# Attention decode with an FFN gate: K loaded ahead of V, the weights placed around them, PV later in the program

## Chip, cores and metric

The kernel runs on one core of a Trainium2 chip. The metric is the device time of one execution in microseconds (us), taken as the median over runs of the same build. The "span" in a profile runs from the first to the last profiled instruction; it lies about 1.8 us below the time of the same run (121.44 against 119.6 before).

Names used below: PE is the TensorE (matmuls and transposes), DVE the VectorE, ACT the ScalarE, SP the engine whose program issues nearly all loads (`SPq` in the views), in the order that is here called the queue. SBUF is the memory on the core, PSUM the one that PE writes to. PV is the product `p @ v`, the FFN is the two products with w1 and w2, and "S7" are the scores of pair 7, the last pair.

## The reference, cut to what matters

```python
# x: [2, 1, 448]; k_cache, v_cache: [2, 8, 8192, 256]; wq: [448, 4096]; wo: [4096, 448]; w1: [448, 1792]; w2: [1792, 448]
xn = layernorm(x)
q  = (xn @ wq) -> [2, 16 heads, 1, 256]
k, v = last 2048 positions of the caches, each of 8 KV heads shared by 2 query heads
p  = softmax(q @ k^T / 16)
s  = (p @ v) @ wo
g  = silu(relu(xn @ w1) @ w2)
out = x + s * g
```

All tensors are bf16. The work is small, the bytes are not: K and V windows 2 x 16.8 MB, wq and wo 2 x 3.7 MB, w1 and w2 2 x 1.6 MB, together 44.1 MB that are each read once.

## The kernel before

The eight KV heads are eight "pairs" (a K and a V of 2 MiB, each loaded as two transfers of 1 MiB, one per batch entry). Per pair, PE transposes K in eight steps (`do_T`), DVE or ACT copy each transposed chunk from PSUM to SBUF ("evacuation"), then come scores (`do_S`), softmax (`ch_*`), PV (`do_PV`, eight steps) and a small output transpose (`do_osb`, `do_oT`). The engines' programs are built step by step: step `8k+s` holds chunk `s` of K of pair `k`, and the other work is hung on later steps. What the whole document turns on: the engines work off these programs in order, so **a piece of work that must wait stops everything behind it on that engine** (the run a_pv_early shows it for PE: transposes whose data had landed stood still for 8.24 us).

```python
NKB, NVB = 3, 4              # buffers for K and V
def load_k(k): d_k[k] = [dma(SP, kbuf[k % NKB], K[k, b], after last_T[k - NKB]) for b in 0, 1]
def load_v(k): d_v[k] = [dma(SP, vbuf[k % NVB], V[k, b], after last_PV[k - NVB]) for b in 0, 1]
# start of the queue: K0 (four half transfers), wq, K1
...
def do_T(i):                 # four PE transposes of one chunk, then its evacuation
    deps = [*landed, p_idf, evac.get(i - 3)]
    ...
    if i % 2 == 0: evac[i] = DVE copy
    else:          evac[i] = ACT copy
...
def do_PV(k, n):             # four matmuls
    deps = [*d_v[k], st["pt", k], ...]
...
at_step(2, 1, do_xr)
at_step(NCH - 1, 1, do_q)                    # NCH = 8
at_step(5 * NCH + 2, 6, do_H)                # FFN: w1
at_step(5 * NCH + 4, 6, do_hT)
at_step(5 * NCH + 6, 6, do_F)                # FFN: w2
for k in range(8):
    e = NCH * k
    at_step(e + 8, 2, do_S(k, 0)); at_step(e + 9, 2, do_S(k, 1))
    at_step(e + 9, 4, ch_max); at_step(e + 11, 4, ch_rmT); at_step(e + 12, 4, ch_bias, ch_exp)
    at_step(e + 15, 4, ch_Pt); at_step(e + 15, 5, ch_sum)
    for n in range(8):
        at_step(e + 17 + n, 3, do_PV(k, n))
    at_step(e + 24, 5, do_osb); at_step(e + 25, 5, do_oT)
# order of the rest of the queue; wo comes last, in four parts
"v0 k2 v1 k3 v2 w1 k4 v3 w2 k5 v4 k6 v5 k7 v6 v7"
...
# after all pairs: at2 (two matmuls, two copies), 128 projection matmuls,
# out = sbk * g + x in two DVE operations, two output DMAs
```

Of the kernel before, what the change touches and what calls it, by code (L numbers as in the profile page):

```python
# [11 lines left out]
PE, DVE, ACTE, SP, POOL = "pe", "dve", "act", "sp", "pool"  # L12
# [64 lines left out]
def bass_recurrent_scan__sliding_block_cached__dense_activation_relu__decode_kernel(  # L77
# [12 lines left out]
    _, HKV, SK, DH = A_k_cache.shape  # L90
# [8 lines left out]
    NT = W // 64  # L99
    NPAIR = HKV  # L100
    NCH = 8
    SLOTS = 7
# [4 lines left out]
    HC = HD // 2  # L107
# [5 lines left out]
    with es:  # L113
        pr = _Prog(nc, es)
# [7 lines left out]
        def view(t, off, dims, n=128, p0=0, pstep=1):  # L122
            width = t.shape[1]
            return bass.AP(t, p0 * width + off, [[width * pstep, n]] + dims)
# [15 lines left out]
        xr = named("xr", [128, SLOTS * 4], BF)  # L140
# [18 lines left out]
        at2 = named("at2", [128, 64], BF)  # L159
        wqo = named("wqo", [128, 32 * D], BF)  # L160
# [3 lines left out]
        kbuf = [named(f"kbuf{i}", [128, NT * DH], BF) for i in range(NKB)]  # L164
# [8 lines left out]
        mbk = mb16[:, :].bitcast(F32).tensor  # L173

        def mbk_ap(lo, n, rows=128):
            return view(mbk, lo, [[1, n]], n=rows)

        def kv_src(k, b, cache):
            return cache[b, k, SK - W:SK, :].rearrange("(m t) d -> m (t d)", t=NT)
# [5 lines left out]
        d_k, d_v = {}, {}  # L185
# [7 lines left out]
        def load_k(k):  # L193
            d_k[k] = [pr.dma(SP, kv_dst(kbuf[k % NKB], b), kv_src(k, b, A_k_cache), [last_T.get(k - NKB)])
                      for b in range(2)]
# [2 lines left out]
            d_v[k] = [pr.dma(SP, kv_dst(vbuf[k % NVB], b), kv_src(k, b, A_v_cache), [last_PV.get(k - NVB)])  # L198
                      for b in range(2)]

        d_k[0] = {}
        for h in range(2):
            for b in range(2):
                lo = h * (NT // 2) * DH
                d_k[0][h, b] = pr.dma((SP, ACTE)[b] if h == 0 else SP,
                                      view(kbuf[0], lo, [[1, NT // 2 * DH]], n=64, p0=b, pstep=2),
                                      kv_src(0, b, A_k_cache)[:, lo:lo + NT // 2 * DH])
        d_x = pr.dma(ACTE, x_sb[0:B, :], A_x[:, 0, :])
        d_xc = [pr.dma(ACTE, view(x_c, 0, [[1, NCOL]], n=4, p0=b, pstep=32),
                       A_x[b, 0, :].rearrange("(i n) -> i n", i=4), [p_xc]) for b in range(B)]  # L210
        d_wq = pr.dma(SP, wqo[:, 0:SLOTS * HC], wq_src)
        load_k(1)

        i0 = pr.op(POOL, lambda e: e.memset(ident[:, :], 0.0))
        p_id = pr.op(POOL, lambda e: e.affine_select(
# [53 lines left out]
        def do_T(i):  # L269
            k, s = divmod(i, NCH)  # L270
            bank, src = tb[i % 3], kbuf[k % NKB]
            src_f, bank_f = src[:, :].bitcast(F32), bank[:, :].bitcast(F32)
            landed = [d_k[0][s // 4, b] for b in range(2)] if k == 0 else d_k[k]
            deps = [*landed, p_idf, evac.get(i - 3)]
            for n in range(4):
                lo = (4 * s + n) * (DH // 2)
                o = pr.op(PE, lambda e, n=n, lo=lo: e.matmul(  # L277
                    bank_f[:, n * 128:(n + 1) * 128], lhsT=src_f[:, lo:lo + 128], rhs=ident_f[:, :],
                    start=True, stop=True, is_transpose=True), deps)
                deps = []  # L280
            last_T[k] = o
            if s == NCH - 1:
                freed.add((load_k, k))
            dst = kt[(i // 2) % (NKT // 2)]
            dst = dst[:, 1024 * (i % 2):1024 * (i % 2) + 1024]
            deps = [o, last_S.get(i - NKT)]
            if i % 2 == 0:
                evac[i] = pr.op(DVE, lambda e: e.tensor_copy(dst, view(bank, 0, [[1, 4], [4, 256]])), deps)  # L288
            else:
                evac[i] = pr.op(ACTE, lambda e: e.activation(dst, view(bank, 0, [[1, 4], [4, 256]]), ACT.Copy), deps)  # L290
# [53 lines left out]
        def ch_sum(k):  # L344
            st["gs", k] = pr.op(PE, mm(mbk_ap(130, 1), gsum[:, :], ssum[k % 2][:, 0:1], True, True),
                                [st["mbk"], v_gs])
            st["rs", k] = st["mbk"] = pr.op(DVE, lambda e: e.reciprocal(rs[:, k:k + 1], mbk_ap(130, 1)), [st["gs", k]])  # L347

        def do_PV(k, n):
            bank, src, p = obk[k % 2], vbuf[k % NVB], pt[k % NP]  # L350
            deps = [*d_v[k], st["pt", k], a_z[2]] + ([st.get(("osb", k - 2)), st["q"]] if n == 0 else [])
            for i in range(4):
                lo = (8 * i + n) * DH
                o = pr.op(PE, mm(bank[32 * i:32 * i + 4, 0:DH], p[:, 16 * n + 4 * i:16 * n + 4 * i + 4],
                                 src[:, lo:lo + DH], n == 0, n == 7, tile_position=(0, 32 * i)), deps)
                deps = []
            last_PV[k] = o
            if n == 7:
                freed.add((load_v, k))

        def do_osb(k):
            st["osb", k] = pr.op(DVE, lambda e: e.tensor_scalar(  # L362
                out=o_sb[k % 2][:, :], in0=obk[k % 2][:, 0:DH], scalar1=rs[:, k:k + 1], scalar2=None, op0=ALU.mult),
                [last_PV[k], st["rs", k], st.get(("oT", k - 2))])
# [12 lines left out]
                    in1=view(qmask, 0, [[0, 2], [0, 2], [1, 4]]), op=ALU.mult), [o, v_qm])  # L377

        def do_q():
            deps = [d_wq, st["xr"], a_z[0]]  # L380
            for s in range(SLOTS):
                for i in range(4):
                    lo = s * HC + i * 512
                    o = pr.op(PE, mm(obk[0][32 * i:32 * i + 4, :], xr[:, 4 * s:4 * s + 4], wqo[:, lo:lo + 512],
                                     s == 0, s == SLOTS - 1, tile_position=(0, 32 * i)), deps)
                    deps = []
            st["q_mm"] = o
            v = pr.op(DVE, lambda e: e.tensor_scalar(
                out=q_n[:, :], in0=obk[0][:, :], scalar1=SCALE, scalar2=None, op0=ALU.mult), [o])
            deps = [v, st["xr"]]  # L390
            for n in range(4):
                o = pr.op(PE, lambda e, n=n: e.matmul(
                    mb16[:, 128 * n:128 * n + 128], lhsT=view(q_n, 256 * (n // 2) + n % 2, [[2, 128]]),
                    rhs=ident[:, :], start=True, stop=True, is_transpose=True), deps)
                deps = []
            for b in range(2):
                for r in range(2):
                    st["q"] = st["mbk"] = pr.op(DVE, lambda e, b=b, r=r: e.tensor_copy(
                        view(qz, 6 * b + r, [[64, 2], [16, 4], [8, 2]]),
                        view(mb16, 256 * r + b, [[2, 2], [32, 4], [128, 2]])), [o, p_qz])  # L400
# [48 lines left out]
        def at_step(i, order, fn):  # L449
            steps.setdefault(i, []).append((order, fn))  # L450

        for i in range(NCH * NPAIR):
            at_step(i, 0, lambda i=i: do_T(i))
        at_step(2, 1, do_xr)
        at_step(NCH - 1, 1, do_q)
        at_step(5 * NCH + 2, 6, do_H)
        at_step(5 * NCH + 4, 6, do_hT)
        at_step(5 * NCH + 6, 6, do_F)
        for k in range(NPAIR):
            e = NCH * k  # L460
            at_step(e + 8, 2, lambda k=k: do_S(k, 0))
            at_step(e + 9, 2, lambda k=k: do_S(k, 1))
            at_step(e + 9, 4, lambda k=k: ch_max(k))
            at_step(e + 11, 4, lambda k=k: ch_rmT(k))
            at_step(e + 12, 4, lambda k=k: ch_bias(k))
            at_step(e + 12, 4, lambda k=k: ch_exp(k))
            at_step(e + 15, 4, lambda k=k: ch_Pt(k))
            at_step(e + 15, 5, lambda k=k: ch_sum(k))
            for n in range(8):
                at_step(e + 17 + n, 3, lambda k=k, n=n: do_PV(k, n))  # L470
            at_step(e + 24, 5, lambda k=k: do_osb(k))
            at_step(e + 25, 5, lambda k=k: do_oT(k))

        loads = []
        for n in "v0 k2 v1 k3 v2 w1 k4 v3 w2 k5 v4 k6 v5 k7 v6 v7".split():
            if n[0] == "w":
                loads.append(((load_w1, load_w2)[int(n[1]) - 1], 0, 1))
            else:
                load, nb = (load_k, NKB) if n[0] == "k" else (load_v, NVB)
                loads.append((load, int(n[1]), nb))  # L480
# [14 lines left out]
        for b in range(2):  # L495
            m_at = pr.op(PE, mm(mbk_ap(256 + 32 * b, 32), at_exp[:, 128 * b:128 * b + 128],
                                fold[:, :], True, True), [st["at", NPAIR - 1, b], v_fold, st["mbk"]])
            v_at2 = st["mbk"] = pr.op(DVE, lambda e, b=b: e.tensor_copy(  # L498
                view(at2, b, [[2, 32]]), mbk_ap(256 + 32 * b, 32)), [m_at])
        deps = [v_at2, st["exp", NPAIR - 1]]  # L500
        landed = dict(d_wo)
        for j in range(32):
# [44 lines left out]
```

## Time and profile before

| | before |
|---|---|
| time, median of 4 runs | 121.57 us (121.25 to 121.86) |
| span of the profiled run | 119.6 us |
| bytes read | 44.1 MB |
| last byte landed | 108.3 us |
| K7 landed / V7 landed | 89.7 / 99.5 us |
| last K transpose done | 101.1 us |
| projection matmuls | 113.4 to 116.5 us |

The first view is the page of the kernel before. The rows of digits are 40 slices of 3 us; each digit is the busy share in tenths. `PEclk` is the clock that the TensorE was granted, in tenths.

```profile
span 119.6 us, 2338 instructions
...
PE   0091953697299989920999359995999899857490
...
PEclk9999679859958999995589985999679999996555
DMA  3998999999999999999999999999999999970000
...
DMA 43%; PE 34%; DVE 6%; ACT 5%; SPq 5%; issue 3%
```

The DMA row is full until slice 35, near 107 us, and then empty for four slices. So the kernel has two limits one after the other: the DMA engines up to 108 us, and then 11 us in which no input byte moves. The PE row has holes in slices 17 to 18 and 22 to 23 (counted from 0), and it is busy again at the end, when the DMA has nothing left to do.

The landing times of the transfers are not in a view of the page; I took them from the trace's records of DMA completions. On SP's queue they come strictly in issue order, one MiB every 2.45 us (428 GB/s). The Trainium skill (DMA: Bandwidth & Descriptors, "Queues, rings and completion order") says less than that: on an engine descriptors are consumed in ring order, but a later one may finish its write before an earlier one. The same page puts the fabric's ceiling at 435 GB/s ("Specifications"), so the queue runs within 2% of it.

The next view is the timeline of PE before, in order of time: start, duration, what ran, and in brackets how long PE sat idle before it and what the profile holds responsible.

```profile
51.42 0.38 PE L255 MATMUL mbk<-ssum,gsum 128*128 128x1 f32 x2 [0.38 <-DVE pt L339]
56.50 1.08 PE L277 MATMUL tb<-ident_f,kbuf 128*128 128x128 f32 x4 [4.69 <-issue]
...
66.73 0.38 PE L255 MATMUL mbk<-ssum,gsum 128*128 128x1 f32 x2 [0.39 <-DVE pt L339]
70.15 0.63 PE L277 MATMUL tb<-ident_f,kbuf 128*128 128x128 f32 x4 [3.04 <-issue]
```

The 4.69 and 3.04 us are put down to "issue", which means that the profile found no releaser. The landing records name it: the second halves of K4 and K5 landed at 56.41 and 70.06, less than 0.1 us before PE went on. (My prediction calls these two K3 and K4; counted from zero they are K4 and K5.) In the queue V2 and w1 stand before K4, and V3 and w2 before K5; a weight takes 3.83 us. The first four transposes of K4 take 1.08 us instead of 0.66: the granted clock was 0.5 there. (Those of K5 took 0.63; its second four took 1.12.)

The last view is the same timeline at the end of the kernel before:

```profile
93.57 0.63 PE L277 MATMUL tb<-ident_f,kbuf 128*128 128x128 f32 x4
...
100.44 0.66 PE L277 MATMUL tb<-ident_f,kbuf 128*128 128x128 f32 x4
...
102.29 0.39 PE L255 MATMUL sbk<-kt,qz 128*4 128x512 bf16 x3
102.84 0.59 PE L255 MATMUL sbk<-kt,qz 128*4 128x512 bf16 x5 [0.16 <-ACT kt L290]
...
107.37 0.36 PE L255 MATMUL mbk<-ident,e_sb 128*128 128x16 bf16 x8 [1.06 <-ACT e_sb L327]
...
109.54 1.67 PE L255 MATMUL obk<-vbuf,pt 128*4 128x256 bf16 x28
...
112.36 0.21 PE L255 MATMUL mbk<-fold,at_exp 128*128 128x32 bf16 x1 [0.35 <-DVE at_exp L374]
...
113.36 3.16 PE L255 MATMUL sbk<-wqo,at 128*2 128x112 bf16 x128 [0.29 <-DVE at L498]
```

`tb<-ident_f,kbuf` are the first and the last transposes of K7, `sbk<-kt,qz` the scores of pair 7, `mbk<-ident,e_sb` the transposes of its probabilities, `obk<-vbuf,pt` PV7, `sbk<-wqo,at` the projection. No line here waits for a DMA: V7 has lain there since 99.5 and wo since 108.3. PE and its partners work off, one after the other, what the late K7 left.

### The profile page before, as it was taken

How to read it: one execution, taken by the hardware profiler on the slowest of the kernel's cores; microseconds unless marked ns; L12 is line 12 of the kernel's file. 1: busy time of each engine (PE TensorE's matmuls, PEld its weight loads, DVE VectorE, ACT ScalarE, POOL GpSimd, SP SyncE). 2: the span in 40 equal slices, each digit the busy share in tenths (PEclk: the TensorE clock that was granted, in tenths of full speed). 3: DMA queues.
4: the chain of work that ended last, by engine and by line, in shares of the span. 5: the costliest groups of instructions: out<-in, count | busy, mean ns of one | idle time of the engine just before them, and what ended most of it. 6: DMA issues, size and time to landing. Idle time of an engine off the chain costs nothing.

```text
span 119.6 us, 2338 instructions
## 1 busy us (share of the span) xinstructions
PE 85.6 (72%) x1015; PEld 53.5 (45%) x1015; DVE 62.9 (53%) x124; ACT 45.6 (38%) x56; POOL 1.8 (2%) x13
## 2 busy tenths in 40 slices
PE   0091953697299989920999359995999899857490
PEld 0081931466145655611456225574466566324280
DVE  0059743449246778720567335886577787424301
ACT  0436640039705656640046503265236566340000
POOL 6000000000000000000000000000000000000000
PEclk9999679859958999995589985999679999996555
DMA  3998999999999999999999999999999999970000
GB/s 49 409 513 365 441 428 433 433 428 428 417 411 428 439 428 419 431 417 417 422 399 453 428 433 411 439 428 417 422 428 428 417 432 406 407 290 11 0 5 3
DMA packets 3902, 44.26 MB, mean 370 GB/s; under 512 B 690, under 2 KB 820, under 8 KB 1204
## 3 DMA queue, kind: packets, MB, share of 16 engines
q1 hardware_dynamic: 3784, 43.58, 86.9%
q10 hardware_dynamic: 108, 0.53, 1.1%
q8 instruction: 8, 0.13, 0.4%
q14 instruction: 2, 0.02, 0.0%
HBM read 44.11 MB, written 0.00 MB: 369 GB/s over the span
## 4 chain that ended last, share of the span: by engine, by line
DMA 43%; PE 34%; DVE 6%; ACT 5%; SPq 5%; issue 3%
DMA kbuf<-in_A_k_cache_dram 43%; PE tb L277 14%; PE sbk L255 9%; PE obk L255 5%; SPq L36 5%; PE mbk L255 4%; ACT e_sb L327 3%; ACT kt L290 2%; PE fbk L255 1%; DVE o_sb L362 1%; DVE kt L288 1%; PE mbk L313 1%; DVE tmp L437 1%; DVE pt L339 1%; DVE rm L308 1%
## 5 line engine op out<-in xcount | busy, mean ns | idle before, releaser
L277 PE MATMUL tb<-ident_f,kbuf 128*128 128x128 f32 x256 | 46.2, 317 | 19.3 <-issue 9.8
L288 DVE COPY kt<-tb 128x1024 bf16<-128x1024 bf16 x32 | 39.0, 1223 | 21.1 <-PE tb L277 20.9
L290 ACT ACTIVATE kt<-tb 128x1024 bf16<-128x1024 bf16 x32 | 32.0, 1021 | 44.9 <-PE tb L277 44.9
L277 PEld LDWEIGHTS tb<-ident_f,kbuf 128*128 128x128 f32 x256 | 32.7, 161 | 27.5 <-issue 23.0
L255 PE MATMUL obk<-vbuf,pt 128*4 128x256 bf16 x256 | 18.5, 303 | 0.0
L255 PE MATMUL sbk<-kt,qz 128*4 128x512 bf16 x128 | 13.3, 490 | 0.2 <-ACT kt L290 0.2
L327 ACT ACTIVATE e_sb<-sbk,bias 128x1024 bf16<-128x1024 f32 x8 | 8.9, 1114 | 10.2 <-DVE bias L323 10.2
L255 PEld LDWEIGHTS obk<-vbuf,pt 128*4 128x4 bf16 x256 | 6.3, 89 | 9.0 <-issue 7.7
L308 DVE TENSOR_REDUCE rm<-sbk 128x1 f32<-128x512 f32 x8 | 5.5, 692 | 7.6 <-PE sbk L255 7.6
L255 PE MATMUL mbk<-ssum,gsum 128*128 128x1 f32 x16 | 3.1, 260 | 4.1 <-DVE pt L339 3.7
L362 DVE TENSOR_SCALAR o_sb<-obk,rs 128x256 bf16<-128x256 f32 x8 | 3.8, 480 | 2.5 <-PE obk L255 2.5
L255 PEld LDWEIGHTS mbk<-ssum,gsum 128*128 128x128 f32 x16 | 2.4, 188 | 4.8 <-DVE pt L339 4.8
L255 PE MATMUL mbk<-ident,e_sb 128*128 128x16 bf16 x64 | 2.9, 171 | 2.1 <-ACT e_sb L327 2.1
L226 DVE BATCH_NORM_STATS2 st<-x_sb 2x6 f32<-2x448 bf16 x1 | 0.6, 616 | 6.8 <-DMA x_sb<-in_A_x_dram 6.8
L255 PEld LDWEIGHTS sbk<-kt,qz 128*4 128x4 bf16 x128 | 2.1, 80 | 4.0 <-issue 3.5
L339 DVE TENSOR_TENSOR pt<-mbk,par 128x128 bf16<-128x128 f32 x8 | 2.3, 291 | 2.6 <-PE mbk L255 2.3
L255 PEld LDWEIGHTS mbk<-ident,e_sb 128*128 128x128 bf16 x64 | 2.1, 96 | 3.3 <-ACT e_sb L327 2.6
L255 PE MATMUL sbk<-wqo,at 128*2 128x112 bf16 x128 | 3.2, 298 | 0.3 <-DVE at L498 0.3
L347 DVE RECIPROCAL rs<-mbk 128x1 f32<-128x1 f32 x8 | 1.3, 169 | 3.8 <-PE mbk L255 3.8
L255 PE MATMUL mbk<-one_f,mrow 1*128 1x1 f32 x16 | 3.0, 256 | 0.3 <-DVE mrow L316 0.2
L255 PEld LDWEIGHTS mbk<-fold,o_sb 128*128 128x128 bf16 x16 | 1.0, 103 | 4.9 <-DVE o_sb L362 3.1
L255 PEld LDWEIGHTS sbk<-wqo,at 128*2 128x2 bf16 x128 | 2.9, 124 | 0.4 <-DVE at L498 0.4
(62 smaller groups left out, 37.5 us busy)
## 6 DMA issues: line engine op xcount, KB each, us to landing
vbuf<-in_A_v_cache_dram SPq DMA_DIRECT2D x16, 1024.0 KB, 26.7
kbuf<-in_A_k_cache_dram SPq DMA_DIRECT2D x14, 1024.0 KB, 25.1
wqo<-in_A_wq_dram SPq DMA_DIRECT2D x1, 3584.0 KB, 14.4
w_sb<-in_B_w_dram SPq DMA_DIRECT2D x2, 1568.0 KB, 33.2
wqo<-in_A_wo_dram SPq DMA_DIRECT2D x1, 1792.0 KB, 17.9
kbuf<-in_A_k_cache_dram SPq DMA_DIRECT2D x3, 512.0 KB, 5.8
wqo<-in_A_wo_dram SPq DMA_DIRECT2D x1, 1120.0 KB, 20.0
kbuf<-in_A_k_cache_dram ACTq DMA_DIRECT2D x1, 512.0 KB, 5.2
```

The costliest lines, as they stand in the source:

```text
L36: o = _Op(eng, lambda e: e.dma_start(dst, src), [d for d in deps if d is not None], True)
L255: return lambda e: e.matmul(out_ap, lhsT=lhsT, rhs=rhs, start=start, stop=stop, skip_group_check=True, **kw)
L277: o = pr.op(PE, lambda e, n=n, lo=lo: e.matmul(bank_f[:, n * 128:(n + 1) * 128], lhsT=src_f[:, lo:lo + 128], rhs=ident_f[:, :], start=True ...
L288: evac[i] = pr.op(DVE, lambda e: e.tensor_copy(dst, view(bank, 0, [[1, 4], [4, 256]])), deps)
L290: evac[i] = pr.op(ACTE, lambda e: e.activation(dst, view(bank, 0, [[1, 4], [4, 256]]), ACT.Copy), deps)
L308: st["rm", k] = pr.op(DVE, lambda e: e.tensor_reduce(out=rm[k % 2][:, :], in_=sbk[:, :], axis=AX.X, op=ALU.max), [st["S", k], st.get(("rmT ...
L313: st["rmT", k] = pr.op(PE, lambda e: e.matmul(mbk_ap(0, 128, 1), lhsT=rm[k % 2][:, :], rhs=ident_f[:, :], start=True, stop=True, is_transp ...
L327: st["exp", k] = pr.op(ACTE, lambda e: e.activation(view(e_sb[k % 2], 0, [[2, 512], [1, 2]]), view(sbk, 0, [[1, 512], [0, 2]]), ACT.Exp, b ...
L339: st["pt", k] = st["mbk"] = pr.op(DVE, lambda e: e.tensor_tensor(out=view(pt[k % NP], 0, [[4, 32], [2, 2], [1, 2]]), in0=view(mbk, 256, [[ ...
L347: st["rs", k] = st["mbk"] = pr.op(DVE, lambda e: e.reciprocal(rs[:, k:k + 1], mbk_ap(130, 1)), [st["gs", k]])
L362: st["osb", k] = pr.op(DVE, lambda e: e.tensor_scalar(out=o_sb[k % 2][:, :], in0=obk[k % 2][:, 0:DH], scalar1=rs[:, k:k + 1], scalar2=None ...
L437: v_rc = pr.op(DVE, lambda e: e.reciprocal(tmp[:, :], ea[:, :]), [v_d])
```

## The change

The intent: keep K far enough ahead of V that PE never waits for a K, and let the last transfers be such that little work follows each of them. The queue becomes wq (first 3/7), K0, wq (rest), K1, K2, V0, K3, V1, and so on to K7, then w1, w2, V5, V6, V7, wo. PV moves with V, three steps later (nine from pair 5 on; the recorded texts say four and ten, but the diff moves it from `e + 17` to `e + 20` and `e + 26`), and the FFN to where w1 and w2 now arrive. Three small things come along: evacuations 3 on DVE to 5 on ACT instead of 4 to 4; the small transpose of x at step 0; one copy for at2 instead of two.

```diff
-        d_k[0] = {}
-        for h in range(2): ...            # K0 in four halves   (cut)
+        d_wq = [pr.dma(SP, wqo[:, 0:3 * HC], wq_src[:, 0:3 * HC])]
+        load_k(0)
+        d_wq.append(pr.dma(SP, wqo[:, 3 * HC:SLOTS * HC], wq_src[:, 3 * HC:SLOTS * HC]))
         load_k(1)
+        load_k(2)
...
-            if i % 2 == 0:
+            if i % 8 in (0, 3, 6):
                 evac[i] = pr.op(DVE, ...)
...
-        at_step(2, 1, do_xr)
+        at_step(0, -1, do_xr)
-        at_step(5 * NCH + 2, 6, do_H)
-        at_step(5 * NCH + 4, 6, do_hT)
-        at_step(5 * NCH + 6, 6, do_F)
+        at_step(8 * NCH + 1, 6, do_H)
+        at_step(8 * NCH + 3, 6, do_hT)
+        at_step(8 * NCH + 5, 6, do_F)
...
+            e += 20 if k < 5 else 26
             for n in range(8):
-                at_step(e + 17 + n, 3, lambda k=k, n=n: do_PV(k, n))
-            at_step(e + 24, 5, lambda k=k: do_osb(k))
-            at_step(e + 25, 5, lambda k=k: do_oT(k))
+                at_step(e + n, 3, lambda k=k, n=n: do_PV(k, n))
+            at_step(e + 7, 5, lambda k=k: do_osb(k))
+            at_step(e + 8, 5, lambda k=k: do_oT(k))
...
-        "v0 k2 v1 k3 v2 w1 k4 v3 w2 k5 v4 k6 v5 k7 v6 v7"
+        "v0 k3 v1 k4 v2 k5 v3 k6 v4 k7 w1 w2 v5 v6 v7"
...                                        # at2: two copies become one   (cut)
```

More of the change, by code (lines that the diff above doesn't have):

```diff
@@ L199, in load_v @@
                       for b in range(2)]
-        d_k[0] = {}
-        for h in range(2):
-            for b in range(2):
-                lo = h * (NT // 2) * DH
-                d_k[0][h, b] = pr.dma((SP, ACTE)[b] if h == 0 else SP,
-                                      view(kbuf[0], lo, [[1, NT // 2 * DH]], n=64, p0=b, pstep=2),
-                                      kv_src(0, b, A_k_cache)[:, lo:lo + NT // 2 * DH])
         d_x = pr.dma(ACTE, x_sb[0:B, :], A_x[:, 0, :])
@@ L210, in bass_recurrent_scan__sliding_block_cached__dense_activation_relu__decode_kernel @@
                        A_x[b, 0, :].rearrange("(i n) -> i n", i=4), [p_xc]) for b in range(B)]
-        d_wq = pr.dma(SP, wqo[:, 0:SLOTS * HC], wq_src)
+        d_wq = [pr.dma(SP, wqo[:, 0:3 * HC], wq_src[:, 0:3 * HC])]
+        load_k(0)
+        d_wq.append(pr.dma(SP, wqo[:, 3 * HC:SLOTS * HC], wq_src[:, 3 * HC:SLOTS * HC]))
         load_k(1)
+        load_k(2)
         i0 = pr.op(POOL, lambda e: e.memset(ident[:, :], 0.0))
@@ L272, in do_T @@
             src_f, bank_f = src[:, :].bitcast(F32), bank[:, :].bitcast(F32)
-            landed = [d_k[0][s // 4, b] for b in range(2)] if k == 0 else d_k[k]
-            deps = [*landed, p_idf, evac.get(i - 3)]
+            deps = [*d_k[k], p_idf, evac.get(i - 3)]
             for n in range(4):
@@ L379, in do_q @@
         def do_q():
-            deps = [d_wq, st["xr"], a_z[0]]
+            deps = [*d_wq, st["xr"], a_z[0]]
             for s in range(SLOTS):
@@ L468, in bass_recurrent_scan__sliding_block_cached__dense_activation_relu__decode_kernel @@
             at_step(e + 15, 5, lambda k=k: ch_sum(k))
+            e += 20 if k < 5 else 26
             for n in range(8):
-                at_step(e + 17 + n, 3, lambda k=k, n=n: do_PV(k, n))
-            at_step(e + 24, 5, lambda k=k: do_osb(k))
-            at_step(e + 25, 5, lambda k=k: do_oT(k))
+                at_step(e + n, 3, lambda k=k, n=n: do_PV(k, n))
+            at_step(e + 7, 5, lambda k=k: do_osb(k))
+            at_step(e + 8, 5, lambda k=k: do_oT(k))
         loads = []
-        for n in "v0 k2 v1 k3 v2 w1 k4 v3 w2 k5 v4 k6 v5 k7 v6 v7".split():
+        for n in "v0 k3 v1 k4 v2 k5 v3 k6 v4 k7 w1 w2 v5 v6 v7".split():
             if n[0] == "w":
@@ L497, in bass_recurrent_scan__sliding_block_cached__dense_activation_relu__decode_kernel @@
                                 fold[:, :], True, True), [st["at", NPAIR - 1, b], v_fold, st["mbk"]])
-            v_at2 = st["mbk"] = pr.op(DVE, lambda e, b=b: e.tensor_copy(
-                view(at2, b, [[2, 32]]), mbk_ap(256 + 32 * b, 32)), [m_at])
+        v_at2 = pr.op(DVE, lambda e: e.tensor_copy(
+            view(at2, 0, [[2, 32], [1, 2]]), view(mbk, 256, [[1, 32], [32, 2]])), [m_at])
         deps = [v_at2, st["exp", NPAIR - 1]]
```

## The prediction

> **What bounds the kernel now.** The page says DMA: 44.1 MB, its engines at 9 tenths in every slice but the first until about 107 us, near 428 GB/s. The landings in the trace's DMA records come strictly in issue order, 2.45 us per MiB, as the Trainium skill says of one ring (DMA: Bandwidth & Descriptors, "Queues, rings and completion order": descriptors on an engine are consumed in ring order). V7 lands at 99.5 us, the last piece of wo at 108.3. But the span is 119.6 us: 11.3 us pass after the last byte. Only the last 3.0 of these (two DVE operations 0.6, output DMA 2.4) must follow it.
>
> The other 8 us are compute that is late. The chain of waits and the timeline show why: PE waits for K3 from 51.8 to 56.5 and for K4 from 67.2 to 70.1, because V, w1 and w2 (3.83 us each) stand in the queue before K3/K4/K5. After 70 us PE is busy almost without a break, 8.65 us per pair at full clock (93.5 to 102.0), 9.5 to 10.6 where the granted clock is 0.5 after an idle stretch. So transposes of K7, landed at 89.7, end at 101; then come, one after the other, the softmax of pair 7 (to 108.1), PV7 (to 111.2), o/at2 (to 113.3), and 128 matmuls of the projection at clock 0.5 (113.4 to 116.5).
>
> **What the change does.** Bytes, buffers and nearly all operations stay. wq first in two pieces around K0; K leads V; w1/w2 after K7. With 2.45 us per MiB I place the landings (estimates from the measured ones): first piece of wq 7.2, K0 12, rest of wq 17, K1 22, K2 27, V0 32, then K and V in turn every 4.9; K7 77, w1 81, w2 84.5, V5 89, V6 94, V7 99.5, wo 104 to 108.3. The DMA end does not move: this is the new floor.
>
> PE: K0's transposes start at 12 instead of 6, q about 24 instead of 20.4. From there a pair of K arrives every 9.8 us and PE needs 8.65 to 10, so T7 ends near 85 to 92 instead of 101. PV is four steps later, matched to V behind K+2. Evacuations go 3:5 to DVE (1.23 us) and ACT (1.02 us) instead of 4:4: about -1.2 us per pair on DVE, +1.0 on ACT; neither binds. The o transposes now fall beside the bias step and may stall PE by some 0.5 us per pair, off the critical path. The FFN (1.6 + 0.9 us PE) and the softmax of pair 7 run while V5 and V6 come in. After V7 at 99.5: PV7 1.7 (cold), o_sb 0.5, transposes and at2 1.3, so ready at about 103, before wo's first part at 103.9. The projection then follows wo's parts; only 8 matmuls come after the last (0.4). End: 108.3 + 0.4 + 3.0 = 111.7 us of span; the time lies 1.85 above the span: **113.5 us** (-6.5%).
>
> **Range** 112.2 to 115.8. Faster by over 2%: 0.97; within: 0.02; slower: 0.01.
>
> **What shows it.** Landings: last wo at about 108.3. Timeline: projection matmuls start near 104, split into four by waits for wo; chain of waits ends in DMA wo, not in PE. No PE wait for K over 3 us after 40 us. Softmax of pair 7 before V6. DMA at 9 tenths from slice 1 to 35.
>
> **What would make it wrong.** PE over 10.5 us per pair (new stalls between DVE and PE, more time at clock 0.5), so that pair 7 is late again; SP issuing a load late because its buffer is freed late (PV later by four steps), leaving the queue empty; a slower stretch of DMA; PV7 and what follows missing wo's first part by over 4 us.

## The result

The changed kernel takes 113.37 us (median of 4 runs, 113.20 to 113.47), against 121.57 us. The ratio is 0.9324 (95% interval 0.9296 to 0.9353). Ratios here and below are the mean time of one kernel's fast runs over that of the other's fast runs in the same rounds, so they are not quite the ratio of the medians quoted.

The page of the changed kernel, the same lines:

```profile
span 111.6 us, 2334 instructions
...
PE   0010699397679789898978979998896677396670
...
PEclk9999999958985999999999999999999999955555
DMA  4999999999999999999999999999999999999920
...
PE 43%; DMA 35%; DVE 7%; issue 6%; ACT 4%; SPq 2%
```

Here a slice is 2.8 us, and the DMA row is full to slice 37. The last byte lands at 108.21 us, as before; the 8 us have gone from behind it. (In all twelve kernels of this document that load every byte it landed between 107.98 and 108.55.) The landing records, in us (second half of each pair):

| | before | predicted | after |
|---|---|---|---|
| K0 / K1 / K2 | 8.6 / 21.9 / 32.9 | 12 / 22 / 27 | 12.0 / 21.8 / 28.0 |
| V0 | 28.2 | 32 | 32.8 |
| K7 | 89.7 | 77 | 77.1 |
| w1 / w2 | 51.5 / 65.1 | 81 / 84.5 | 80.9 / 84.8 |
| V5 / V6 / V7 | 84.8 / 94.6 / 99.5 | 89 / 94 / 99.5 | 89.7 / 94.6 / 99.5 |
| wo, first / last part | 103.9 / 108.3 | 104 / 108.3 | 103.8 / 108.2 |

The timeline of PE in the changed kernel, from pair 7 to the end:

```profile
79.52 0.64 PE L272 MATMUL tb<-ident_f,kbuf 128*128 128x128 f32 x4
...
88.43 1.13 PE L251 MATMUL sbk<-kt,qz 128*4 128x512 bf16 x16
89.29 1.69 PE L251 MATMUL fbk<-w_sb,xr 128*4 128x256 bf16 x28
...
94.58 0.36 PE L251 MATMUL mbk<-ident,e_sb 128*128 128x16 bf16 x8 [0.38 <-ACT e_sb L322]
...
97.82 2.18 PE L251 MATMUL obk<-vbuf,pt 128*4 128x256 bf16 x32
100.07 0.21 PE L251 MATMUL mbk<-fold,o_sb 128*128 128x4 bf16 x2
100.22 1.66 PE L251 MATMUL obk<-vbuf,pt 128*4 128x256 bf16 x28
...
103.04 0.23 PE L251 MATMUL mbk<-fold,at_exp 128*128 128x32 bf16 x2 [0.35 <-DVE at_exp L369]
103.92 1.66 PE L251 MATMUL sbk<-wqo,at 128*2 128x112 bf16 x64 [0.65 <-DMA wqo<-in_A_wo_dram]
106.60 2.02 PE L251 MATMUL sbk<-wqo,at 128*2 128x112 bf16 x64 [1.02 <-DMA wqo<-in_A_wo_dram]
```

Pair 7 starts at 79.52 instead of 93.57, its scores at 88.43 instead of 102.29. The FFN (`fbk<-w_sb,xr`) runs behind them. The projection now waits for wo, part by part, where before wo waited for it.

The chain of waits, in order of time, ends so (start, duration, what):

```profile
76.07 30.48 DMA wqo<-in_A_wo_dram
106.55 0.04 issue
106.60 1.62 PE sbk L251 x49
108.22 0.04 issue
108.26 0.39 PE sbk L251 x8
108.64 0.02 issue
108.67 0.29 DVE tmp L505
108.95 0.02 issue
108.98 0.27 DVE out_sb L507
```

Read this with care. The page's summary gives PE 43% of the chain, which looks PE-bound. But the chain ends in a load of wo, and the 30.48 us of that load run from its issue to its landing: nearly all of it is waiting in the queue, since V7 was still landing at 99.48. Before 76 us the chain follows what released the *issue* of that load (V7's buffer, freed by PV3), and those are the PE shares. That issue was more than 20 us early, so the PE time in the chain cost nothing. What the chain shows of the end is right: behind the last byte stand 8 matmuls, two DVE operations and the output.

### The profile page after: what moved, and what is told of

Its sections match the earlier page's. It is cut to its first block, busy times and chain, and to the rows that moved or that the text cites. A ratio compares the mean times of both kernels' runs of the same rounds, so it can differ in the third digit from the quotient of the medians.

```text
span 111.6 us, 2334 instructions
## 1 busy us (share of the span) xinstructions
PE 79.6 (71%) x1015; PEld 51.4 (46%) x1015; DVE 54.3 (49%) x115; ACT 54.0 (48%) x64; POOL 1.8 (2%) x13
## 4 chain that ended last, share of the span: by engine, by line
PE 43%; DMA 35%; DVE 7%; issue 6%; ACT 4%; SPq 2%
DMA wqo<-in_A_wo_dram 27%; PE tb L272 23%; PE sbk L251 9%; DMA kbuf<-in_A_k_cache_dram 7%; PE obk L251 5%; PE mbk L251 5%; DVE kt L283 3%; ACT kt L285 2%; SPq L36 2%; DVE pt L334 1%; ACT L322 1%; ACT e_sb L322 1%; DVE mrow L311 1%; DVE q_n L383 1%; DVE bias L318 0%
## 5 line engine op out<-in xcount | busy, mean ns | idle before, releaser
L285 ACT ACTIVATE kt<-tb 128x1024 bf16<-128x1024 bf16 x40 | 40.3, 1022 | 32.1 <-PE tb L272 32.1
L272 PE MATMUL tb<-ident_f,kbuf 128*128 128x128 f32 x256 | 41.6, 297 | 7.4 <-issue 7.1
L283 DVE COPY kt<-tb 128x1024 bf16<-128x1024 bf16 x24 | 29.4, 1225 | 23.4 <-PE tb L272 23.4
L272 PEld LDWEIGHTS tb<-ident_f,kbuf 128*128 128x128 f32 x256 | 30.3, 151 | 16.6 <-issue 14.0
L251 PE MATMUL obk<-vbuf,pt 128*4 128x256 bf16 x256 | 16.9, 304 | 0.1
L251 PE MATMUL sbk<-kt,qz 128*4 128x512 bf16 x128 | 11.5, 433 | 0.0
L251 PEld LDWEIGHTS mbk<-one_f,mrow 1*128 1x128 f32 x16 | 2.3, 182 | 5.2 <-DVE mrow L311 5.1
L251 PE MATMUL mbk<-fold,o_sb 128*128 128x4 bf16 x16 | 1.7, 173 | 2.4 <-DVE bias L318 1.3
L369 DVE TENSOR_TENSOR at_exp<-mbk,qmask 128x16 bf16<-128x16 f32 x16 | 2.0, 169 | 2.4 <-PE mbk L251 2.4
```

What stands on the lines that cost most here:

```text
L251: return lambda e: e.matmul(out_ap, lhsT=lhsT, rhs=rhs, start=start, stop=stop, skip_group_check=True, **kw)
L272: o = pr.op(PE, lambda e, n=n, lo=lo: e.matmul(bank_f[:, n * 128:(n + 1) * 128], lhsT=src_f[:, lo:lo + 128], rhs=ident_f[:, :], start=True ...
L283: evac[i] = pr.op(DVE, lambda e: e.tensor_copy(dst, view(bank, 0, [[1, 4], [4, 256]])), deps)
L285: evac[i] = pr.op(ACTE, lambda e: e.activation(dst, view(bank, 0, [[1, 4], [4, 256]]), ACT.Copy), deps)
L369: st["at", k, b] = st["mbk"] = pr.op(DVE, lambda e, b=b: e.tensor_tensor(out=view(at_exp, 128 * b + 16 * k, [[8, 2], [4, 2], [1, 4]]), in0 ...
```

## The experiments

Eleven kernels ran; all gave results within the comparison's tolerance. "b_" starts from the kernel before, "a_" from the changed kernel. The last three columns are from the traces (start of K7's transposes, of pair 7's scores "S7", of the projection), so each is of one execution. That execution was the fastest of its kernel for b_w_late_pv (113.94 us), b_k_lead (114.78) and a_dve6 (128.12), and a slow one for a_pv_early.

| run | what | time, us | ratio to before | K7 starts | S7 | projection |
|---|---|---|---|---|---|---|
| (before) | | 121.57 | 1 | 93.6 | 102.3 | 113.4 |
| (after) | | 113.37 | 0.9324 | 79.5 | 88.4 | 103.9 |
| b_w_late | w1, w2 after K7, FFN there | 116.09 | 0.951 | 82.5 | 91.2 | 108.6 |
| b_k_lead | K ahead, PV later | 115.66 | 0.9467 | 86.0 | 95.2 | 107.7 |
| b_evac | 3:5 only | 120.74 | 0.9905 | 93.1 | 102.3 | 112.8 |
| b_wq_first | start only | 121.20 | 0.9937 | 93.4 | 102.1 | 113.4 |
| b_pv_late | PV later only | 123.01 | 1.0074 | 93.8 | 102.9 | 115.7 |
| b_w_late_pv | b_w_late and PV later | 114.89 | 0.9432 | 82.3 | 91.4 | 107.4 |
| a_no_lead | change without K ahead | 114.21 | 0.9373 | 82.0 | 90.9 | 106.5 |
| a_pv_early | change with PV as before | 120.76 | 0.9845 | 79.0 | 99.9 | 113.0 |
| a_evac44 | change with 4:4 | 113.25 | 0.9307 | 77.8 | 87.0 | 103.7 |
| a_less_w2 | 0.8 MB less of w2 | 111.20 | 0.9139 | 78.1 | 87.0 | 102.4 |
| a_dve6 | 6:2 on DVE | 131.23 | (128.12 fast) | 93.1 | 106.1 | 121.6 |

My theory at the outset: the last byte at 108.2 is the floor, and the gain is that K7 is done in time. Rivals: the gain lies in the balance of the evacuations; in the start; in one of the two reorderings alone.

### b_w_late: only w1 and w2 moved, with the FFN

```diff
-at_step(5 * NCH + 2, 6, do_H) ... do_hT ... do_F
+at_step(8 * NCH + 1, 6, do_H) ... do_hT ... do_F
-"v0 k2 v1 k3 v2 w1 k4 v3 w2 k5 v4 k6 v5 k7 v6 v7"
+"v0 k2 v1 k3 v2 k4 v3 k5 v4 k6 v5 k7 w1 w2 v6 v7"
```

> The kernel before with one thing of the change: w1 and w2 queued after K7 and the FFN run at steps 65 to 69; K does not lead V further, PV, wq and evacuations as before. Theory (what counts is only that the last K is transposed and its softmax done before V7 lands; the rest of the change is spare): K7 lands near 82 us instead of 89.7, the last transpose is done by about 92 instead of 101, last byte at 108.3 as ever, time 113.3 to 114.8. Rival (the lead of K over V, with PV later, is needed): K7 comes 7.7 us earlier but PE still stalls on V in order, time 116 to 119.

Measured: 116.09 us (115.33 to 116.53), ratio 0.951 (0.9463 to 0.9556). K7 landed at 82.4 and the last transpose was done at 90.0 (the theory said 82 and 92); the time was at the rival's lower edge. The timeline of PE shows where the rest went:

```profile
92.25 0.59 PE L255 MATMUL sbk<-kt,qz 128*4 128x512 bf16 x5
95.04 0.32 PE L255 MATMUL obk<-vbuf,pt 128*4 128x256 bf16 x4 [2.20 <-DMA vbuf<-in_A_v_cache_dram]
...
98.50 0.22 PE L255 MATMUL fbk<-ident,h_n 128*128 128x16 bf16 x2 [0.67 <-DVE mrow L316]
...
108.62 3.15 PE L255 MATMUL sbk<-wqo,at 128*2 128x112 bf16 x128 [0.29 <-DVE at L498]
```

The first matmuls of PV6 stand in PE's program before the softmax of pair 7 and before the FFN, and wait for V6 (landed at 94.9). So the move of the weights is a large part of the gain, about 5.9 of 8.2 us, but not all of it, and the theory's "the rest is spare" fell.

### b_k_lead: only K ahead, with PV later; the weights stay in the middle

```diff
         load_k(1)
+        load_k(2)
-"v0 k2 v1 k3 v2 w1 k4 v3 w2 k5 v4 k6 v5 k7 v6 v7"
+"v0 k3 v1 k4 v2 w1 k5 v3 w2 k6 v4 k7 v5 v6 v7"
+e += 20 if k < 5 else 26          # PV, osb, oT as in the change
```

> The kernel before with K2 loaded before V0, K two pairs further ahead in the queue, PV later as in the change; but w1 and w2 stay in the middle of the queue (after V2 and V3) and the FFN at steps 42 to 46; wq and evacuations as before. Theory (spare on both sides): K7 lands near 84.5, last transpose about 93, softmax of pair 7 done before V7 at 99.5, time 113.3 to 115. Rival (the weights in the middle of the queue are the cause of the late end): PE still waits 3 to 5 us for a K behind each weight and the FFN delays pair 5, time 117 to 121.

Measured: 115.66 us (114.78 to 115.89), ratio 0.9467 (0.9425 to 0.9509). Neither number was met: it lies between the theory's range and the rival's. K7 landed at 84.9, the last transpose was done at 93.8, and the projection could start only at 107.65 with all of wo's first part there since 104. Each of the two reorderings alone gives 5% and they overlap: together they give 6.8%. Both bring K7 forward, by 7.3 us and 4.8 us against before; once the projection waits for wo, a still earlier pair 7 brings nothing (a_evac44 below: S7 1.5 us earlier, the same time).

### b_evac: only the evacuations 3:5

```diff
-            if i % 2 == 0:
+            if i % 8 in (0, 3, 6):
```

> The kernel before with only the evacuations split 3 on DVE to 5 on ACT of each eight. Theory (neither engine binds, PE does): within 1% of before, 120.5 to 122.3; a pair of K costs PE 8.6 to 9.4 us after 84 us. Rival (DVE at 53% busy was holding up PE, and relieving it is a good part of the gain): below 119.5.

Measured: 120.74 us (120.63 to 121.18), ratio 0.9905 (0.9872 to 0.9938), as the theory had it. The last transpose ends at 101.06 (before: 101.09). The 0.6 us appear only after it: the scores of pair 7 no longer wait for ACT's last evacuation, and the projection starts at 112.8 instead of 113.4. The rival is out.

### b_wq_first: only the start

```diff
-K0 in four halves, wq in one transfer, do_xr at step 2
+wq (3/7), K0, wq (4/7), do_xr at step 0, x first on ACT's queue
```

> The kernel before with only the start of the change: wq in two pieces around K0, K0 whole, x first on its queue, the small transpose of x at step 0. Theory (the start has slack: K1 lands at the same time, so PE resumes at the same time): first transpose near 12 instead of 6 us, S0 at 22.5 as before, time 120.8 to 122.2. Rival (an earlier end of the start-up is part of the gain): below 120.

Measured: 121.20 us (121.12 to 121.37), ratio 0.9937 (0.9915 to 0.9959). K0's transposes start at 12.05 instead of 6.05, K1's at 21.87 instead of 21.97: six microseconds later at the start, and nothing is left of it one pair on. The time fell by 0.6%, which is measured but was not traced to a place; the end of the trace looks like that of before.

### b_w_late_pv: b_w_late, and PV later

```diff
 (b_w_late)
+            e += 20 if k < 5 else 26
```

> b_w_late with one thing more, PV later as in the change (4 steps, 10 from pair 5 on); still no further lead of K over V, evacuations and start as before. b_w_late ended at 114.7 us of span because S7's softmax and the FFN stand in PE's program behind the first matmuls of PV6, which waited for V6 at 94.9. Theory (that order in PE's program is what was missing): softmax 7 and FFN are done by about 97, projection starts with wo's first part near 104, time 113.2 to 114.3. Rival (the lead of K itself is needed for the rest): stays at 115 to 116.5.

Measured: 114.89 us (113.94 to 115.55), ratio 0.9432 (0.9369 to 0.9496): between the two. The wait for V6 before the softmax is gone, PE goes from S7 at 91.4 straight on, yet the projection starts at 107.4. The work from S7 to the projection (FFN, softmax 7, PV5, PV6, PV7, at2) takes PE and its partners 16 us, so S7 would have to be near 88 to meet wo. The order in PE's program was part of what was missing, not all. Two cautions: the intervals of this ratio and of b_w_late's overlap (0.9369 to 0.9496, 0.9463 to 0.9556), so the part that PV's place gives here is barely clear of noise; and the profiled run was the fastest of the four, because its projection ran at full clock, 1.74 us instead of the 3.15 in b_w_late's trace. At the half clock the same trace would have ended 1.4 us later, an estimate that accounts for most of the spread of this kernel's runs (113.94 to 115.55).

### a_pv_early: the changed kernel with PV at its old steps

```diff
-            e += 20 if k < 5 else 26
+            e += 17
```

> The changed kernel with PV at its old place, 17 steps after the pair's first transpose, for all pairs. Theory (PE runs its program in order, so a PV that stands before its V has landed stops the transposes behind it): PV5 stands among the transposes of K7 and waits for V5 at 89.7, PV6 stands before the softmax of pair 7 and waits for V6 at 94.6; last transpose near 97 instead of 87, projection from about 107 on, time 115.5 to 119. Rival (PV's place is a side matter, the order of the loads does it all): 113.2 to 114.

Measured: 120.76 us (119.06 to 122.21), ratio 0.9845 (0.9754 to 0.9935, from its two fast runs, 119.06 and 120.61). The direction is the theory's and the rival is out, but the loss is larger than the range. The timeline of PE in the profiled run (120.90 us; it is 1.5% above the fastest of this kernel and so counts as slow):

```profile
80.78 0.60 PE L251 MATMUL sbk<-kt,qz 128*4 128x512 bf16 x8
89.62 0.38 PE L251 MATMUL obk<-vbuf,pt 128*4 128x256 bf16 x4 [8.24 <-DMA vbuf<-in_A_v_cache_dram]
...
90.01 1.09 PE L272 MATMUL tb<-ident_f,kbuf 128*128 128x128 f32 x4
```

PE had K7 (landed 76.9) and could have gone on transposing, but four matmuls of PV5 stood before and waited 8.24 us for V5. The Trainium skill says that only weight loads are pulled ahead, while "The MATMULs themselves stay in program order" (TensorE: Matmul & The Clock Gate, Part 2, "Step-by-step: what each phase is for"); this trace agrees. What I had not put into the range is the second line: after the wait, four transposes took about 1.1 us instead of 0.66, up to 98.5. The granted clock was 0.55 on average from 90 to 100 us. The same page ("HAM oscillation — how this bites in real kernels") warns of PE idle gaps above about 3.4 us, after which PE runs at the half clock; this gap of 8.24 us was followed by it. But the half clock came after much shorter gaps too: in the changed kernel it was granted from 97.4 us on, and no gap of PE in the 60 us before that was longer than 1.44 us. So 3.4 us is no safe limit here. The wait for V5 follows from the landing of V5 and does not depend on the run's state; how much of the low clock belongs to the slow state I can't say, since no fast run of this kernel was profiled; the two fast runs list mean clocks of 0.914 and 0.898, no higher than the 0.914 of the profiled one. The order of the queue without the order of PE's program to match it keeps about 1.9 of the 8 us (0.8 to 3.0 by the interval; against before the verdict is "unclear", against the change the loss of over 5 us is clear).

### a_evac44: the changed kernel with evacuations 4:4

```diff
-            if i % 8 in (0, 3, 6):
+            if i % 2 == 0:
```

> The changed kernel with evacuations shared 4:4 again. Theory (off the critical path, spare of 3 to 4 us before V7): a pair costs PE about 9.6 us instead of 9.38, last transpose 1 to 2 us later, time unchanged, 113.1 to 113.9. Rival (the 3:5 split carries a part of the gain, as b_evac's 1% hints): 114.3 or more.

Measured: 113.25 us (113.20 to 113.48), ratio 0.9307: no different from the change. A pair costs PE 9.62 us against 9.38, as expected. The last transpose is nevertheless 1.5 us *earlier* than in the change (85.6 against 87.0), since in this run pair 2 ran at a better clock (8.28 against 10.13 us from pair 2's start to pair 3's). And it does not matter: the projection waits for wo in both.

The waits of PE, in us, times, longest, first in the changed kernel and then with 4:4:

```profile
PE mbk L251 <- DVE mrow L311: 3.7, 7, 0.9
...
PE mbk L251 <- DVE bias L318: 1.3, 5, 0.3
```

```profile
PE mbk L251 <- DVE bias L318: 4.9, 5, 1.1
...
PE mbk L251 <- DVE mrow L311: 0.7, 2, 0.5
```

These are small DVE operations of the softmax that stand behind a 1.2 us evacuation in DVE's order. The split decides which of them is held up.

### a_less_w2: half of w2's bytes (a wrong result)

```diff
-w2_src = ...rearrange("(hf p j) n -> p hf (j n)", hf=2, j=7)
+w2_src = ...rearrange("(hf p j) n -> p hf (j n)", hf=2, j=7)[:, 0, :]
-lo = f * D + i * NCOL
+lo = (f % 7) * D + i * NCOL
```

> The changed kernel loading only the first half of w2 and using it twice (a wrong result on purpose): 0.80 MB less in the queue, nothing else moved. Theory (the end is set by the last byte): w2 took 3.83 us, so everything after it lands 1.9 us earlier, the last part of wo near 106.3, time 111.2 to 111.8. Rival (compute has taken over the end): 112.6 to 113.5.

Measured: 111.20 us (111.10 to 111.42), ratio 0.9139. (The result stayed within the comparison's tolerance although half of w2 was not read; the kernel is not valid for that.) a_evac44 ran beside it on the same chip and is as fast as the change, so it is the better measure: the last part of wo landed at 106.04 against 107.98 there, 1.94 us earlier, and the time is 111.20 against 113.25, 2.05 us less. The time follows the last byte one for one. The rival is out.

### a_no_lead: the changed kernel without the further lead of K

```diff
-        load_k(2)
-"v0 k3 v1 k4 v2 k5 v3 k6 v4 k7 w1 w2 v5 v6 v7"
+"v0 k2 v1 k3 v2 k4 v3 k5 v4 k6 v5 k7 w1 w2 v6 v7"
```

> The changed kernel without the further lead of K: K2 after V0, each V before the K two pairs on, as before; w1 and w2 still after K7, PV late, start and 3:5 evacuations kept. It differs from b_w_late_pv only in start and evacuations, from the change only in the lead. Theory (K7 five us later in the queue eats the spare that PE had before V7): K7 lands near 82, S7 near 91 instead of 88.4, time 114.2 to 115.6. Rival (the rest of b_w_late_pv's loss lay in its start and evacuations): 113.1 to 113.8.

(One correction to that text: this kernel differs from b_w_late_pv also in the single at2 copy.) Measured: 114.21 us (114.02 to 114.35), ratio 0.9373 (0.9334 to 0.9413), as the theory had it. The end of PE's timeline:

```profile
90.94 1.12 PE L250 MATMUL sbk<-kt,qz 128*4 128x512 bf16 x16
...
106.49 2.95 PE L250 MATMUL sbk<-wqo,at 128*2 128x112 bf16 x128 [0.32 <-DVE at L493]
```

S7 is 2.5 us later than in the change, the projection starts 2.6 us later and no longer waits for wo, and the time is 0.84 us longer (113.37 and 114.21 are of different rounds; by the two ratios to before it is 0.6 us, with intervals that just overlap; in the traces the projection ends at 109.44 instead of 108.61). So the changed kernel had about 1.7 us to spare at S7 (2.5 less 0.84), no more. Both S7 are of one execution each, and it varies with the clock (a_less_w2, in the same order, has it at 87.0). But the trace of the change gives nearly the same by itself: its projection ended at 108.61, and in one go at the half clock it took 3.16 us before, so it could have started at 105.45 instead of 103.92; with the 0.3 us that it had waited for wo's first part this makes 1.9 us, an estimate. The 0.7 us between this kernel and b_w_late_pv are not clear of noise (the intervals overlap).

### a_dve6: the changed kernel with six of eight evacuations on DVE

```diff
-            if i % 8 in (0, 3, 6):
+            if i % 4 != 1:
```

> The changed kernel with six of each eight evacuations on DVE, to see how much spare there is. DVE then has 6 x 1.23 + 2.3 = 9.7 us of work per pair. Theory (spare before the end shows is small, about 1.5 to 2 us at S7): a pair costs 10 to 10.6 us, S7 near 92 to 94, time 114.5 to 117. Rival (wide spare, as my prediction had it: harmless up to 10.5 us per pair): 113.1 to 113.9.

Measured: 131.23 us median, 128.12 in its one fast run; far above both. The pairs from 3 on took 11.6, 12.2, 13.6 and 13.6 us. PE's waits in this run:

```profile
PE mbk L251 <- DVE pt L334: 9.9, 8, 1.9
PE mbk L251 <- DVE mrow L311: 6.8, 7, 1.6
...
PE mbk L251 <- DVE bias L318: 6.1, 5, 1.2
```

I had added up DVE's work per pair (9.7 us) and left out the order in which it stands: the softmax's short operations (0.15 to 0.3 us each) queue behind one or two evacuations, and PE waits for each of them in order. 22.8 us of such waits (9.9 + 6.8 + 6.1) stand against 9.6 in the change, where `pt` took 4.6 and the other two are shown above. As a test of the spare it was too coarse; a_no_lead answers that question.

### b_pv_late: only PV later, with the old queue

```diff
+            e += 20 if k < 5 else 26
```

> The kernel before with only PV later. Theory (alone it moves nothing that the late K7 holds up): K7 still lands at 89.7 with FFN in pair 5, last transpose 99 to 101, time 120 to 122.5. Rival (PV among the transposes was what made PE late): below 119.

Measured: 123.01 us, ratio 1.0074 (1.0001 to 1.0148); its profiled run is fast, but at 123.67 us the slowest of the three fast ones. K7 starts at 93.8 as before, and the projection 2.3 us later than before: more PV work stands behind the late scores of pair 7, and the moved `do_oT` now waits for the bias copy (0.94 to 1.15 us a pair in its timeline). PV later is worth nothing by itself, it only pays together with the queue.

## Why the prediction was right

**The floor.** Predicted: the last byte stays at 108.3, and after it come 0.4 us of matmuls and 3.0 us of DVE and output; span 111.7, time 113.5. Measured: 108.21, span 111.6, time 113.37. a_less_w2 shows that this is the limit now: take 1.9 us from the last byte and the time loses 2.05 us.

**Where the 8 us came from.** Predicted: compute that was late because K stood behind V, w1 and w2. The experiments confirm it and divide it, though not into a sum: the weights' move alone gives 4.9% of the time, K's lead with PV later alone 5.3%, both with the small things 6.8%. PV's place is a condition: without it the new queue keeps 1.6% (0.7 to 2.5), and alone it gains nothing (0.7% longer). One effect for which the prediction had no number goes the same way: the same 1015 matmuls kept PE busy for 79.6 us instead of 85.6, while the mean granted clock from 5 to 105 us was 0.93 instead of 0.88. No run separates what the fewer idle stretches did by themselves from what the clock added. The start and the evacuations are worth 0.6% and 1% on the old kernel; with 4:4 evacuations the changed kernel is as fast.

**PE's pace.** Predicted 8.65 to 10 us per pair, with some 0.5 us of stall by the moved output transposes; measured 9.38 us, with waits of 0.38 and 0.25 us at the bias step in most pairs.

**Steps whose size was off, without effect on the time:**

- "q about 24": q was ready at 21.4, and the scores of pair 0 started at 22.5, behind K1's first transposes. I let q wait for more than it does; the q matmuls ran at 18.04, right after the rest of wq (landed 16.9) and K0's last transposes.
- "Softmax of pair 7 before V6": the probability transposes came at 94.58, V6 landed at 94.57. DVE was then busy with the silu, so `pt` followed at 96.0. So it was slightly late.
- "After V7 at 99.5: PV7 ...": the sum met 103 for the readiness of at2, but for another reason. PE was still at PV6 and its output transpose until 100.22, 0.7 us after V7. In this run the end of the compute was set by PE's own program from S7 on, and not by V7; that the sum met 103 is luck. (In a_evac44, with S7 1.5 us earlier, V7 did set it: PE waited 0.99 us for it.) One term that I left out helped here: at2 with one copy instead of two takes about 0.5 us less (from its first matmul to readiness 1.0 us before, 0.5 after).
- "PE over 10.5 us per pair" as the threshold for going wrong: too generous. From the spare of 1.7 us found by a_no_lead and the five pairs (3 to 7) that PE does without waiting for a K, the threshold works out near 9.38 + 1.7/5 = 9.7 us per pair. That is an estimate; no run has that pace with the change's order. The prediction's range held because the pace was 9.38, not because the spare was wide.

Open: where b_wq_first's 0.6% comes from.

None of the variants beats the changed kernel by more than their spread (a_evac44 113.25 against 113.37), and a_less_w2 says why none could: the order of bytes is used up, only fewer bytes or less work behind the last one would help.

## What to carry to other kernels

Where all bytes are needed and the queue is always full, the end of the last byte is fixed; so ask of each load how much work must follow it, load first what has a long chain behind it (K), last what has a short one (wo), and put once-used weights where nothing waits behind them. Then move the consumers in each engine's program to match the queue: an instruction that waits for a late load stops independent work behind it, and here (a_pv_early) that took back most of the gain. Judge spare time by delaying one thing by a known amount, not by adding up an engine's busy time.

## What the Trainium skill lacked or had wrong

- Runtime: NRT & Kernel Launch, "Instruction fetch mechanics", calls the cost of crossing a 16 KiB boundary "mostly hidden"; it does not say what the fetch does to loads that are under way. In the traces these fetches are packets of 16,384 bytes on the same DMA engines, eight per run. The first one after the queue is full stood at 25.9 us in the changed kernel (26.0 before), and the K or V transfer that was landing then needed 3.8 us instead of 2.45 (24.28 to 28.04; before 24.33 to 28.19); the later landings hardly caught up (the next took 2.29). In a_dve6 the fetch came at 26.9 and the late landing moved to another transfer (26.97 to 30.08). The cause is argued from this coincidence, not tested, and it was only the first fetch: beside the later ones no landing of K or V in the changed kernel took more than 2.63 us.
- DMA: Bandwidth & Descriptors gives in "Specifications" an HBM limit per core of about 358 GB/s, and its "Where 436 GB/s comes from" says that for HBM to SBUF this side binds. One core alone moved a mean of 425 GB/s from 5 to 105 us in the changed kernel, near the 435 GB/s that the page gives for the fabric. (Its "Measured" part does list 425 GB/s for a single core, and says that about 358 is what each gets when both cores of a pair stream; the other two places leave this condition out.)
- No page that I read goes beyond finding what an idle engine waits for, to the case of b_w_late and a_pv_early, a matmul that waits for a load and so holds up work behind it that is ready: PE idle for 2.20 and 8.24 us with a load of V as the releaser, while the softmax of pair 7, or K7's transposes, could have run. TensorE: Matmul & The Clock Gate has the rule (program order), not this consequence for placing loads.
